# Reordering the start of a fused windowed-attention and feed-forward kernel: maxima one step ahead, early hidden slices in banks of their own, weights converted in another order

## The chip, the cores and the metric

The kernel runs on one core of one Trainium2 chip. The metric is device time in microseconds: the median of a few executions. One further execution was taken with the hardware profiler; all single durations come from it, and the profile's times count from the start of its span.

## What is computed

```python
# q, k, v: (8, 8, 576, 64); window = 32, dilation = 4
scores = (q @ k.T) / sqrt(64)
# heads 0-3: 0 <= i - j < 32;  heads 4-7: 0 <= i - j < 128 and (i - j) % 4 == 0
attn = softmax(where(mask, scores, -1e9))
x = (attn @ v).transpose(0, 2, 1, 3).reshape(4608, 512)   # tokens x model
h = x @ w_in                                              # w_in: 512 x 2048
g = maximum(h, 0) + alpha * minimum(h, 0)                 # alpha: one number per hidden unit
out = g @ w_out                                           # w_out: 2048 x 512
```

All is float32. Each large product is made of three matmuls in a rounded type (`PASSES`): every factor is split into a high part (rounded) and a low part (the rest), and high x high, high x low and low x high are added up in PSUM.

## The kernel before

**Work units.** A *pair* is two heads of one batch element: 32 pairs, 0 to 31, four (`NC`) for each batch element. A pair goes through `scores` (TensorE, 72 small matmul records, into two PSUM banks), `maxima` (VectorE: scale, mask, row maximum), `exponentials` (ScalarE, nine with their sums), `divisions` and `turns` (VectorE: divide, transpose), `values` (TensorE, into two banks), `highs` (ScalarE) and `lows` (VectorE), which write the split result into the token tiles x. Tokens come in nine tiles of 512.

**The feed-forward part** works in *slices* (t, f): token tile t, 128 hidden units f. `ffn_h` is 12 matmuls into one bank; `ffn_relu` makes two relus (ScalarE); `ffn_sum` joins them with alpha (VectorE); `ffn_high` (ScalarE) and `ffn_low` (VectorE) split g; `ffn_y` is 12 matmuls that add to four banks y. The list `slices` begins with (0, 0) to (0, 5) (`CUT` is 6), then (1, 0) to (1, 15), then the rest of tile 0 and tile 2. After slice 5 the four banks y are emptied: `end()` in `ffn_y` copies each to a buffer `o[c]` (ScalarE for c = 0 and 2, VectorE for c = 1 and 3) and stores it to `part`. It is called one step later, at n = 6, through `ended`.

**Weights** arrive as 64-bit numbers. One *conversion* (32 in all: `w_in` and `w_out`, 16 chunks each) is a load, `magnitude` (two ScalarE operations into a buffer `a`), `words` (two VectorE operations), `high` (ScalarE) and `low` (VectorE). `wq` sets their order, `taken` how many begin in each step. A conversion that begins in step n has its words and high in step n + 1 and its low in step n + 2 (lists `now` and `late`).

**Buffers around the change.** There are eight PSUM banks, a0 to a3 and y0 to y3; `bank` gives them out in turn. The tag "m" has five buffers of 128 x 512, used by the relu results, by the copies `o[c]`, and by the buffer `a` of conversions, unless `magnitude` takes `spare_a`:

```python
i = self.index                      # place in wq
if NC <= i < 2 * HALF and i % 2 == 0:       # NC = 4, HALF = 8
    self.a = spare_a[i // 2 % 2]
else:
    self.a = ffp.tile([P, DM], U32, tag="m", name=f"wa{self.id}", bufs=5)
```

**Order.** All five engines run in the order in which the program names their operations (`manual_schedule`); an operation waits only for its data and for its buffer to come free, and all behind it on its engine wait too. SP issues all DMAs. The start of the program handles pairs 0 to 4 in a loop over s, a loop over n = 0 to 5 the pairs up to 7 together with slices 0 to 5, and a loop over n from 6 on the other slices and more pairs. The last six token tiles follow in a stage of their own, which the change leaves as it is.

Of the kernel before, what the change touches and what calls it, by code (L numbers as in the profile page):

```python
# [15 lines left out]
ALU = mybir.AluOpType  # L16
# [37 lines left out]
def tile_window_attention_prelu_ffn(  # L54
# [34 lines left out]

    turn = {"a": 0, "y": 0, "g": 0}  # L90

    def bank(side, shape, name):
        n = turn[side]
        turn[side] = n + 1
        return psp.tile(shape, F32, tag=f"{side}{n % 4}", name=name)

    def gbuf(shape, dtype, name, i=None):
# [52 lines left out]
    class Pair:  # L150
        def __init__(self, b, c):
            self.b, self.c = b, c
            p = b * NC + c
            self.banks = "y" if p <= NC else "a"
            self.plain = 2 * c < HP
            self.mask = PLAIN if self.plain else DILATED
            self.id = f"{b}_{c}"
            self.pr = spare_pr[p % 2] if b < 2 else pr0
            self.room = rooms[c] if b < 2 else None
            self.sm = sums[p % 2]  # L160
# [63 lines left out]
        def values(self):  # L224


            self.po = [bank("a", [P, HB, BQ], f"o_{self.id}_{u}") for u in range(2)]
            for i in range(HB + 1):
                a, z = max(0, i - 1), min(HB, i + 1)
                for u in range(2):  # L230
                    if u == 0 and i == 0:
                        continue
                    for e in range(2):
                        rows = slice((2 * e + u) * BQ, (2 * e + u + 1) * BQ)
                        nc.tensor.matmul(  # L235
                            self.po[u][e * D:(e + 1) * D, a:z, :], lhsT=self.v[rows, i, :],
                            rhs=self.pt[rows, a * BK + (BQ if i else 0):z * BK - (BQ if i <= HB - 1 else 0)],
                            start=i == 1 - u, stop=i == HB, skip_group_check=True)
# [95 lines left out]


    gs, ys, ms = {}, {}, {}
    PASSES = ((0, 0), (0, 1), (1, 0))

    def ffn_h(t, f, first=0, end=NC):
        if first == 0:  # L340
            ms[t, f] = bank("a", [P, TT], f"h_{t}_{f}")
        for c in range(first, end):
            for n, (a, e) in enumerate(PASSES):
                nc.tensor.matmul(  # L344
                    ms[t, f], lhsT=weight(0, a, f)[:, c * P:(c + 1) * P], rhs=half(t, c)[:, e, :],
                    start=(c == 0 and n == 0), stop=(c == NC - 1 and n == 2))

    def ffn_relu(t, f):

        ps = ms[t, f]  # L350
        m = ffp.tile([P, TT], F32, tag="m", name=f"m_{t}_{f}", bufs=5)
        nc.scalar.activation(out=m, in_=ps, func=AF.Relu, scale=-1.0)
        nc.scalar.activation(out=ps, in_=ps, func=AF.Relu)
        ms[t, f] = ps, m

    def ffn_sum(t, f):
        ps, m = ms[t, f]
        nc.vector.scalar_tensor_tensor(
            out=m, in0=m, scalar=nal[:, f:f + 1], in1=ps, op0=ALU.mult, op1=ALU.add)
        ms[t, f] = m  # L360
# [8 lines left out]
    def ffn_high(t, f):  # L369
        g = gbuf([P, 2, TT], F32R, f"g_{t}_{f}")  # L370
        nc.scalar.copy(out=g[:, 0, :], in_=ms[t, f])  # L371
        gs[t, f] = g

    def ffn_low(t, f):
        g = gs[t, f]
        nc.vector.tensor_tensor(out=g[:, 1, :], in0=ms.pop((t, f)), in1=g[:, 0, :].bitcast(F32), op=ALU.subtract)

    def ffn_y(t, f):
        first = (t, f) in ((0, 0), (0, CUT), (1, 0), (2, HALF))
        if first:  # L380
            ys[t] = [bank("y", [P, TT], f"y_{t}_{f}_{c}") for c in range(NC)]
        g = gs.pop((t, f))
        cut, rest = (t, f) == (0, CUT - 1), t == 0 and f == NF - 1
        last = cut or (t, f) in ((0, NF - 1), (1, NF - 1), (2, HALF - 1))
        if last:
            o = [ffp.tile([P, TT], F32, tag="m", name=f"ob_{t}_{f}_{c}", bufs=5) for c in range(NC)]
        for c in range(NC):
            if rest:
                nc.sync.dma_start(out=o[c], in_=part[c])
            for n, (a, e) in enumerate(PASSES):  # L390
                nc.tensor.matmul(  # L391
                    ys[t][c], lhsT=weight(1, a, f)[:, c * P:(c + 1) * P], rhs=g[:, e, :],
                    start=(first and n == 0), stop=(last and n == 2),
                )

        def end():
            for c in range(NC):
                if rest:
                    nc.vector.tensor_tensor(out=o[c], in0=ys[t][c], in1=o[c], op=ALU.add)
                elif c % 2:  # L400
                    nc.vector.tensor_copy(out=o[c], in_=ys[t][c])
                else:
                    nc.scalar.copy(out=o[c], in_=ys[t][c])  # L403
                nc.sync.dma_start(
                    out=part[c] if cut else outT[c * P:(c + 1) * P, t * TT:(t + 1) * TT], in_=o[c])

        if last:
            ended.append(end)
# [363 lines left out]
    pairs = [Pair(b, c) for b in range(B) for c in range(NC)]  # L772


    wq = [(0, 0), (0, 1), (1, 0)]
    for f in range(1, NF):
        wq += [(0, f + 1), (1, f)] if f + 1 < NF else [(1, f)]
    order.update({w: i for i, w in enumerate(wq)})
    loads, convs = list(wq), list(wq)

    def load():
        if loads:
            load_weight(*loads.pop(0))
# [7 lines left out]
    def masks_of(kind):  # L791
        nc.sync.dma_start(out=mask_sb[:, kind:kind + HB], in_=masks[:, kind:kind + HB])
# [2 lines left out]
    pairs[0].load_qk()  # L795
    masks_of(PLAIN)
    load()
    nc.sync.dma_start(out=al, in_=alpha)
    pairs[1].load_qk()
    load()  # L800
    pairs[0].load_v()
    pairs[2].load_qk()
    load()
    pairs[1].load_v()
    masks_of(DILATED)
    pairs[3].load_qk()
    load()
    pairs[2].load_v()
# [5 lines left out]
    pairs[0].exponentials()  # L814
    for op in w.words():
        op()
    nc.vector.tensor_scalar_mul(nal, al, -1.0)
    nc.vector.tensor_scalar(out=bal, in0=al, scalar1=-1.0, scalar2=1.0, op0=ALU.mult, op1=ALU.add)
    w.high()
    before, w = w, conversion()  # L820
    for s in range(NC):
        u = pairs[s]
        pairs[s + NC].load_qk()
        load()
        if s + 1 == NC:
            ffn_h(0, 0, 0, 2)
            ffn_h(0, 1, 0, 2)
        pairs[s + 1].maxima()
        if s:
            pairs[s - 1].highs()  # L830
        pairs[s + 1].exponentials()
        if s:
            for op in w.words():
                op()
            w.high()
            later = conversion()
            pairs[s - 1].lows()
        u.divisions()
        u.turns()
        if s == 0:  # L840
            for op in w.words():
                op()
            w.high()
            later = conversion()
        before.low()
        before, w = w, later
        if s + 1 == NC:
            ffn_h(0, 0, 2, 3)
            ffn_h(0, 1, 2, 3)
        if s + 2 <= NC:  # L850
            pairs[s + 2].scores()
        u.values()
        pairs[s + NC].load_v()
    u, v = pairs[NC - 1], pairs[NC]
    u.highs()
    v.divisions()
    u.lows()
    for f in range(2):
        ffn_h(0, f, NC - 1, NC)
    v.turns()  # L860
    for op in w.words():
        op()
    ffn_relu(0, 0)
    ffn_relu(0, 1)
    before.low()
    w.high()
    load()
    late, now = [w], [conversion()]

    taken = [1, 2, 1, 1, 1, 2] + [1, 1, 2, 1, 1, 1, 2, 1, 1, 2, 1, 2, 1]  # L870

    def ahead():
        while taken and len(convs) - taken[0] < len(loads):
            load()

    for n in range(CUT):
        scored = pairs[NC + 1 + n] if n + 1 < NC else None
        valued = pairs[NC + n] if n < NC else None
        if n == 0:
            for f in range(2):  # L880
                ffn_sum(*slices[f])
        elif n > 1:
            ffn_sum(*slices[n])
        if scored:
            scored.scores()
        if valued:
            valued.values()
        if n:
            ffn_h(*slices[n + 1])
        ffn_high(*slices[n])  # L890
        if scored:
            scored.maxima()
            scored.exponentials(0, 5)
        ffn_low(*slices[n])
        if valued:
            valued.highs()
        if scored:
            scored.exponentials(5)
        if n:
            ffn_relu(*slices[n + 1])  # L900
        for w in now:
            for op in w.words():
                op()
        if valued:
            valued.lows()
        for w in late:
            w.low()
        if scored:
            scored.divisions()
            scored.turns()  # L910
        for w in now:
            w.high()
        late, now = now, [conversion() for _ in range(taken.pop(0))]
        ahead()
        if n:
            ffn_y(*slices[n - 1])

    score_at, value_at = {}, {}
    for p in range(2 * NC, AHEAD):
# [152 lines left out]
```

## Time and profile before

| | |
|---|---|
| median of 3 runs | 882.77 us (880.36 to 882.95) |
| profiled execution | 881.63 us, span 879.5 us |
| mean granted TensorE clock | 0.986 |
| TensorE busy | 850.5 us (97%), 8048 matmuls |
| VectorE busy | 536.1 us (61%), 901 instructions |
| ScalarE busy | 415.8 us (47%), 1150 instructions |
| GpSimd busy | 46.9 us (5%) |
| HBM read, written | 116.98 MB, 33.55 MB |

A row of the time line has the start in us, the duration in us, the engine, the line, the operation, output <- inputs, partitions x elements and type, the count, and in brackets the idle time before it with what ended it. A row of the chain has start, duration and what. The page shows each engine in 40 slices of 22 us, a digit being the busy share in tenths. "Granted clock" is the share of its full clock that TensorE had.

### The profile page before, as it was taken

What the parts mean: (1) busy time and instruction counts of PE and PEld (TensorE: products, weight loads), DVE (VectorE), ACT (ScalarE), POOL (GpSimd) and SP (SyncE); (2) the same over time, 40 slices, a digit from 0 to 9 for tenths busy, and PEclk for the clock granted to TensorE, in tenths of its full rate; (3) what the DMA queues carried; (4) which work ended last, traced back from release to release, by engine and by line L of the source; (5) the groups of instructions that cost most, each with busy time, mean ns of one, the idle gap of its engine ahead of it and who ended that gap; (6) DMA issues with size and microseconds to landing.
All of it is one profiled execution on the core that took longest, in us unless ns stands there. A gap on an engine that the chain in (4) does not pass through costs nothing.

```text
span 879.5 us, 19618 instructions
## 1 busy us (share of the span) xinstructions
PE 850.5 (97%) x8048; PEld 702.6 (80%) x8048; DVE 536.1 (61%) x901; ACT 415.8 (47%) x1150; POOL 46.9 (5%) x52
## 2 busy tenths in 40 slices
PE   4789999999999999999999999999999999999998
PEld 4577888888888788888888888888788888888886
DVE  6987677676776778674447665754277637304721
ACT  7886777534334344553446443643264226204500
POOL 0000000200504440000000000000000000000000
PEclk9779999999999999999999999999999999999999
DMA  9713344126889963765566666655475467435641
GB/s 338 250 67 120 120 162 144 48 95 208 270 294 313 286 192 124 240 179 151 163 178 198 172 175 193 192 145 158 113 193 145 147 194 194 121 96 172 182 126 48
DMA packets 95304, 151.81 MB, mean 173 GB/s; under 512 B 8432, under 2 KB 39152, under 8 KB 95216
## 3 DMA queue, kind: packets, MB, share of 16 engines
q1 hardware_dynamic: 95216, 150.57, 56.3%
q8 instruction: 63, 1.03, 0.5%
q14 instruction: 25, 0.20, 0.1%
HBM read 116.98 MB, written 33.55 MB: 171 GB/s over the span
## 4 chain that ended last, share of the span: by engine, by line
PE 95%; DMA 2%; issue 1%; DVE 1%; SPq 0%; ACT 0%; DVEq 0%
PE y L679 30%; PE h L344 15%; PE y L391 15%; PE pA L541 15%; PE pC L541 7%; PE o L235 5%; PE s L189 4%; PE pB L541 4%; DMA mask_sb<-masks 1%; DMA ws<-w_in 1%; DVE x L276 0%; DVE pt L222 0%; DVE wa L321 0%; DVE w_dt.float L197 0%; DVE w_dt.float L216 0%
## 5 line engine op out<-in xcount | busy, mean ns | idle before, releaser
L344 PE MATMUL h<-x,w_dt.float32r 128*128 128x512 f32 x576 | 144.5, 400 | 2.6 <-ACT x L271 1.2
L391 PE MATMUL y<-g,w_dt.float32r 128*128 128x512 f32 x576 | 138.7, 390 | 0.0
L344 PEld LDWEIGHTS h<-x,w_dt.float32r 128*128 128x128 f32 x576 | 109.0, 192 | 26.7 <-issue 1.6
L391 PEld LDWEIGHTS y<-g,w_dt.float32r 128*128 128x128 f32 x576 | 107.8, 188 | 23.0 <-ACT ob L403 0.4
L679 PE MATMUL y<-gp,ring_w 128*128 128x512 f32 x480 | 112.3, 390 | 0.0
L679 PEld LDWEIGHTS y<-gp,ring_w 128*128 128x128 f32 x480 | 89.7, 188 | 18.9
L679 PE MATMUL y<-gp,ring_xA 128*128 128x512 f32 x444 | 103.9, 390 | 0.0
L679 PEld LDWEIGHTS y<-gp,ring_xA 128*128 128x128 f32 x444 | 83.0, 188 | 17.6
L207 ACT ACTIVATE pr<-pr,nm 128x64 f32<-128x64 f32 x216 | 72.2, 336 | 45.7 <-DVE nm L200 45.7
L583 ACT COPY stage<-pA 128x512 f32<-128x512 f32 x72 | 42.3, 587 | 105.2 <-PE pA L541 105.2
L371 ACT CAST g<-m 128x512 fp32r<-128x512 f32 x48 | 29.7, 619 | 74.4 <-DVE m L366 71.6
L609 DVE TENSOR_TENSOR gp<-n,gp 128x512 fp32r<-128x512 f32 x96 | 63.2, 684 | 0.0
L601 DVE SCALAR_TENSOR_TENSOR n<-n,bal,stage 128x512 f32<-128x512 f32 x72 | 53.9, 749 | 13.9 <-ACT n L597 13.1
L541 PE MATMUL pA<-parts_w,ring_w 128*128 128x512 f32 x234 | 57.7, 390 | 0.7 <-ACT raw_xA L271 0.7
L605 ACT CAST gp<-n 128x512 fp32r<-128x512 f32 x96 | 56.6, 615 | 1.8 <-DVE n L601 1.8
L541 PE MATMUL pA<-parts_w,ring_xA 128*128 128x512 f32 x228 | 56.2, 390 | 0.5 <-ACT raw_xB L271 0.5
L679 PE MATMUL y<-gp,ring_g 128*128 128x512 f32 x228 | 54.5, 391 | 0.0
L541 PEld LDWEIGHTS pA<-parts_w,ring_w 128*128 128x128 f32 x234 | 43.8, 188 | 9.9 <-ACT raw_xA L271 0.8
L702 DVE TENSOR_TENSOR ob<-y,py 128x512 f32<-128x512 f32 x24 | 16.4, 691 | 57.8 <-PE y L679 57.8
L597 ACT ACTIVATE n<-stage 128x512 f32<-128x512 f32 x72 | 45.6, 633 | 12.5 <-DVE stage L590 12.0
L541 PEld LDWEIGHTS pA<-parts_w,ring_xA 128*128 128x128 f32 x228 | 42.7, 188 | 9.4 <-ACT raw_xB L271 0.6
L679 PEld LDWEIGHTS y<-gp,ring_g 128*128 128x128 f32 x228 | 42.5, 188 | 9.1
(96 smaller groups left out, 1139.8 us busy)
## 6 DMA issues: line engine op xcount, KB each, us to landing
ring_w<-wS SPq DMA_DIRECT2D x68, 256.0 KB, 2.9
ring_xA<-wS SPq DMA_DIRECT2D x67, 256.0 KB, 2.9
ring_w<-wO SPq DMA_DIRECT2D x40, 256.0 KB, 2.8
ring_xA<-wO SPq DMA_DIRECT2D x37, 256.0 KB, 2.7
out<-ob SPq DMA_DIRECT2D x36, 256.0 KB, 3.0
ring_g<-wS SPq DMA_DIRECT2D x33, 256.0 KB, 2.9
wO<-w_dt.float32r SPq DMA_DIRECT2D x32, 256.0 KB, 4.8
wS<-wc SPq DMA_DIRECT2D x16, 512.0 KB, 4.1
```

Source lines behind the costliest of these rows:

```text
L189: nc.tensor.matmul(self.ps[j // CUT0][m * BQ:(m + 1) * BQ, j % CUT0, :], lhsT=self.q[rows, n * BQ:(n + 1) * BQ], rhs=keys, start=True, sto ...
L207: nc.scalar.activation(out=self.pr[:, r, :], in_=self.pr[:, r, :], func=AF.Exp, bias=self.nm[:, r:r + 1], scale=1.0, accum_out=self.sm[:, ...
L235: nc.tensor.matmul(self.po[u][e * D:(e + 1) * D, a:z, :], lhsT=self.v[rows, i, :], rhs=self.pt[rows, a * BK + (BQ if i else 0):z * BK - (B ...
L344: nc.tensor.matmul(ms[t, f], lhsT=weight(0, a, f)[:, c * P:(c + 1) * P], rhs=half(t, c)[:, e, :], start=(c == 0 and n == 0), stop=(c == NC ...
L391: nc.tensor.matmul(ys[t][c], lhsT=weight(1, a, f)[:, c * P:(c + 1) * P], rhs=g[:, e, :], start=(first and n == 0), stop=(last and n == 2),)
L541: nc.tensor.matmul(to, lhsT=w[:, (2 * a + c) * P:(2 * a + c + 1) * P], rhs=part_of(name, e)[:, c * TT:(c + 1) * TT], start=start and c == ...
L583: nc.scalar.copy(out=self.s(n), in_=self.A)
L597: nc.scalar.activation(out=self.m[n], in_=self.at(n), func=AF.Relu, scale=-1.0)
L601: nc.vector.scalar_tensor_tensor(out=self.m[n], in0=self.m[n], scalar=bal[:, f:f + 1], in1=self.at(n), op0=ALU.mult, op1=ALU.add)
L605: nc.scalar.copy(out=self.g(n)[:, 0], in_=self.m[n])
L609: nc.vector.tensor_tensor(out=g[:, 1], in0=self.m.pop(n), in1=g[:, 0].bitcast(F32), op=ALU.subtract)
L679: nc.tensor.matmul(ys2[tt], lhsT=w[:, k * P:(k + 1) * P], rhs=g[:, e], start=j == 0 and n == 0, stop=j == GF - 1 and n == 2)
```

## The change

- `maxima` and `exponentials` of pairs 5, 6 and 7 come one step earlier: ahead of the `divisions` of the pair before. Their `scores` come earlier too, in the banks y.
- The h of slices 2 to 6 get banks a2 and a3 (`early`), values of pairs 4 to 7 banks a0 and a1. `ffn_h` runs up to three slices ahead of `ffn_y`.
- `wq` and `taken` change: chunks of `w_in` for tile 0 come first; two conversions a step from n = 2 to 5, then one and two in turn.
- Alpha is loaded and prepared later; the second set of masks is loaded one weight chunk and one v earlier.

```diff
-    def bank(side, shape, name):
-        n = turn[side]
-        turn[side] = n + 1
+    def bank(side, shape, name, n=None):
+        if n is None:
+            n = turn[side]
+            turn[side] = n + 1
...
-            self.banks = "y" if p <= NC else "a"
+            self.banks = "y" if p < 2 * NC else "a"
...
+                bank("a", [P, HB, BQ], f"o_{self.id}_{u}", u if NC <= self.p < 2 * NC else None) for u in range(2)]
...
+    early = [(0, f) for f in range(2, CUT)] + [(1, 0)]
...
+            ms[t, f] = bank("a", [P, TT], f"h_{t}_{f}", 2 + (t + f) % 2 if (t, f) in early else None)
...
-    wq = [(0, 0), (0, 1), (1, 0)]
-    for f in range(1, NF):
-        wq += [(0, f + 1), (1, f)] if f + 1 < NF else [(1, f)]
+    wq = [(0, 0), (0, 1), (1, 0), (0, 2), (0, 3), (0, 4), (1, 1), (0, 5)] + [(1, f) for f in range(2, CUT)]
+    wq += [(a, f) for f in range(CUT, NF) for a in range(2)]
...
-    nc.sync.dma_start(out=al, in_=alpha)          # was between the first two weight loads
+    masks_of(DILATED)                             # ahead of the third load; was behind v of pair 1
...
     for s in range(NC):
...
         if s + 1 == NC:
+            nc.sync.dma_start(out=al, in_=alpha)
             ffn_h(0, 0, 0, 2)
             ffn_h(0, 1, 0, 2)
...
-        if s + 2 <= NC:
-            pairs[s + 2].scores()
+        pairs[s + 2].scores()
         u.values()
...
     u.highs()
-    v.divisions()
+    pairs[NC + 1].maxima()
     u.lows()
     for f in range(2):
         ffn_h(0, f, NC - 1, NC)
+    v.divisions()
     v.turns()
     for op in w.words():
         op()
+    nc.vector.tensor_scalar_mul(nal, al, -1.0)
+    nc.vector.tensor_scalar(out=bal, in0=al, scalar1=-1.0, scalar2=1.0, op0=ALU.mult, op1=ALU.add)
     ffn_relu(0, 0)
     ffn_relu(0, 1)
+    pairs[NC + 2].scores()
     before.low()
+    pairs[NC + 1].exponentials()
     w.high()
...
-    taken = [1, 2, 1, 1, 1, 2] + [1, 1, 2, 1, 1, 1, 2, 1, 1, 2, 1, 2, 1]
+    taken = [1, 1, 2, 2, 2, 2] + [1, 2, 1, 2, 1, 2, 1, 2, 1, 2]
```

The loop over n from 0 to 5, new:

```python
for n in range(CUT):
    scored, divided, valued = (pairs[p] if p < 2 * NC else None for p in (NC + 2 + n, NC + 1 + n, NC + n))
    summed = [k for k in ((0, 1) if n == 0 else (n + 1,)) if k < CUT]
    if not divided:
        for w in late: w.low()
    for k in summed: ffn_sum(*slices[k])
    if valued: valued.values()
    if n == 0:
        ffn_h(*slices[2])
        pairs[2 * NC - 1].scores()
    if n < 2: ffn_h(*slices[n + 3])
    if summed: ffn_high(*slices[summed[0]])
    if scored: scored.maxima()
    if valued: valued.highs()
    if scored: scored.exponentials()
    if summed: ffn_low(*slices[summed[0]])
    if n == 0: ffn_high(*slices[1])
    if n + 2 < CUT or n + 1 == CUT: ffn_relu(*slices[min(n + 2, CUT)])
    for w in now:
        for op in w.words(): op()
    if valued: valued.lows()
    if divided:
        for w in late: w.low()
        divided.divisions(); divided.turns()
    if n == 0: ffn_low(*slices[1])
    for w in now: w.high()
    late, now = now, [conversion() for _ in range(taken.pop(0))]
    ahead()
    if n: ffn_y(*slices[n - 1])
    if n in (2, 3): ffn_h(*slices[n + 3])
```

More of the change, by code (lines that the diff above doesn't have):

```diff
@@ L152, in __init__ @@
             self.b, self.c = b, c
-            p = b * NC + c
-            self.banks = "y" if p <= NC else "a"
+            p = self.p = b * NC + c
+            self.banks = "y" if p < 2 * NC else "a"
             self.plain = 2 * c < HP
@@ L224, in values @@
         def values(self):
-            self.po = [bank("a", [P, HB, BQ], f"o_{self.id}_{u}") for u in range(2)]
+            self.po = [
+                bank("a", [P, HB, BQ], f"o_{self.id}_{u}", u if NC <= self.p < 2 * NC else None) for u in range(2)]
             for i in range(HB + 1):
@@ L340, in ffn_h @@
         if first == 0:
-            ms[t, f] = bank("a", [P, TT], f"h_{t}_{f}")
+            ms[t, f] = bank("a", [P, TT], f"h_{t}_{f}", 2 + (t + f) % 2 if (t, f) in early else None)
         for c in range(first, end):
@@ L802, in tile_window_attention_prelu_ffn @@
     pairs[2].load_qk()
+    masks_of(DILATED)
     load()
     pairs[1].load_v()
-    masks_of(DILATED)
     pairs[3].load_qk()
@@ L816, in tile_window_attention_prelu_ffn @@
         op()
-    nc.vector.tensor_scalar_mul(nal, al, -1.0)
-    nc.vector.tensor_scalar(out=bal, in0=al, scalar1=-1.0, scalar2=1.0, op0=ALU.mult, op1=ALU.add)
     w.high()
@@ L876, in tile_window_attention_prelu_ffn @@
     for n in range(CUT):
[L877 to L885, printed above, removed]
+        scored, divided, valued = (pairs[p] if p < 2 * NC else None for p in (NC + 2 + n, NC + 1 + n, NC + n))
+        summed = [k for k in ((0, 1) if n == 0 else (n + 1,)) if k < CUT]
+        if not divided:
+            for w in late:
+                w.low()
+        for k in summed:
+            ffn_sum(*slices[k])
         if valued:
             valued.values()
-        if n:
-            ffn_h(*slices[n + 1])
-        ffn_high(*slices[n])
+        if n == 0:
+            ffn_h(*slices[2])
+            pairs[2 * NC - 1].scores()
+        if n < 2:
+            ffn_h(*slices[n + 3])
+        if summed:
+            ffn_high(*slices[summed[0]])
         if scored:
             scored.maxima()
-            scored.exponentials(0, 5)
-        ffn_low(*slices[n])
         if valued:
@@ L897, in tile_window_attention_prelu_ffn @@
         if scored:
-            scored.exponentials(5)
-        if n:
-            ffn_relu(*slices[n + 1])
+            scored.exponentials()
+        if summed:
+            ffn_low(*slices[summed[0]])
+        if n == 0:
+            ffn_high(*slices[1])
+        if n + 2 < CUT or n + 1 == CUT:
+            ffn_relu(*slices[min(n + 2, CUT)])
         for w in now:
@@ L905, in tile_window_attention_prelu_ffn @@
             valued.lows()
[L906 to L910, printed above, removed]
+        if divided:
+            for w in late:
+                w.low()
+            divided.divisions()
+            divided.turns()
+        if n == 0:
+            ffn_low(*slices[1])
         for w in now:
@@ L916, in tile_window_attention_prelu_ffn @@
             ffn_y(*slices[n - 1])
+        if n in (2, 3):
+            ffn_h(*slices[n + 3])
     score_at, value_at = {}, {}
```

## The prediction

> **What bounds the kernel now.** I read the page's slices, the chain that ended last, the stretches, then each engine in order of time up to 101 us. First the row of slices; two stretches (window, length, busy us and count of PE, PE loads, VectorE, ScalarE, GpSimd, then granted clock, DMA share, GB/s); pieces of the chain (start, us, what):
>
> ```profile
> PE   4789999999999999999999999999999999999998
> 40.00:57.74 17.74, 13.15 (x309) 11.16 (x310) 16.57 (x36) 14.38 (x54) 0.00 (x0) 0.62 0.36 117
> 71.52:97.58 26.06, 26.06 (x185) 21.78 (x186) 17.12 (x28) 17.27 (x32) 0.00 (x0) 1.00 0.19 71
> ...
> 71.52 1.35 PE o L235 x70
> 81.27 2.72 PE y L391 x12
> 83.98 2.72 PE h L344 x12
> 97.58 3.08 PE y L391 x12
> 100.66 0.46 PE h L344 x2
> ```
>
> From 71.52 us TensorE is full at clock 1.00, and both kernels give it the same work. So the question is when it reaches the same place of its list. Before that VectorE is nearly full (16.57 of 17.74 us), and TensorE waits for it at clock 0.62. Slices are numbered as in `slices` (h6, y6 belong to slice 6), conversions c0, c1, ... in order of `wq`, pairs 0 to 7.
>
> **The start.** Alpha leaves the front of SP's queue and the dilated masks pass one weight load. That removes VectorE's wait for masks (first row). What is late next is the magnitude of c2: ScalarE ends it at 17.97 + 0.72 = 18.69, so words of c2 move from 18.87 only to 18.7, and all behind them by 0.2.
>
> ```profile
> 17.16 0.49 DVE L197 SCALAR_TENSOR_TENSOR w_dt.float<-s,mask_sb 128x320 f32<-128x320 f32 x1 [0.81 <-DMA mask_sb<-masks]
> 18.87 0.75 DVE L321 SCALAR_TENSOR_TENSOR wa<-ws,wa 128x512 uint16<-128x512 uint16 x1
> ...
> 17.97 0.72 ACT L314 ACTIVATE wa<-wa,least 128x512 int32<-128x512 int32 x1
> 43.09 0.60 ACT L329 CAST w_dt.float32r<-wa 128x512 fp32r<-128x512 f32 x1
> ...
> 36.71 1.35 PE L235 MATMUL o<-pt,w_dt.float 32*64 32x32 f32 x76
> 47.69 1.21 PE L189 MATMUL s<-w_dt.float 64*32 64x64 f32 x72
> ```
>
> Values of pair 3 ended at 36.71 + 1.35 = 38.06. Scores of pair 5 (1.2) now stand ahead of them: 39.1. Highs, lows, the last chunk of h0 and h1 and both relus follow as before, so relu 1 ends not at 43.1 but at 44.1. VectorE's maxima of pair 5 stand ahead of those lows, but end before highs are there; its divisions 4, words c5, the two alpha operations and sums are through by 46, under ScalarE's queue. The masks' and weights' DMAs land before their users; the weight behind the masks (c2) has until 17.28, where ScalarE now takes it.
>
> **ScalarE, then VectorE, to sum 5.** The durations are distances between starts (VectorE, then ScalarE), and one group row (busy, mean ns):
>
> ```profile
> 55.50 0.88 DVE L276 TENSOR_TENSOR x<-o,x 128x288 fp32r<-128x288 f32 x3
> 56.29 0.69 DVE L332 TENSOR_TENSOR w_dt.float32r<-w_dt.float,w_dt.float32r 128x512 fp32r<-128x512 f32 x1
> 62.41 0.49 DVE L197 SCALAR_TENSOR_TENSOR w_dt.float<-s,mask_sb 128x320 f32<-128x320 f32 x1 [1.59 <-PE s L189]
> 64.13 0.68 DVE L376 TENSOR_TENSOR g<-m,g 128x512 fp32r<-128x512 f32 x1
> 64.72 0.76 DVE L321 SCALAR_TENSOR_TENSOR w_dt.float<-w_dt.uint,w_dt.float 128x512 uint16<-128x512 uint16 x1
> 66.12 0.76 DVE L321 SCALAR_TENSOR_TENSOR wa<-w_dt.uint,wa 128x512 uint16<-128x512 uint16 x1
> 67.53 1.36 DVE L276 TENSOR_TENSOR x<-o,x 128x224 fp32r<-128x224 f32 x4
> 68.79 0.69 DVE L332 TENSOR_TENSOR w_dt.float32r<-wa,w_dt.float32r 128x512 fp32r<-128x512 f32 x1
> 69.39 0.17 DVE L214 TENSOR_SCALAR rs<-sums 128x9 f32<-128x9 f32 x1
> 71.34 0.70 DVE L358 SCALAR_TENSOR_TENSOR m<-m,nal,h 128x512 f32<-128x512 f32 x1
> ...
> 87.75 0.61 ACT L329 CAST w_dt.float32r<-w_dt.float 128x512 fp32r<-128x512 f32 x1
> 88.26 0.66 ACT L313 ACTIVATE wa<-w_dt.uint 128x512 f32<-128x512 bf16 x1
> 89.58 0.66 ACT L313 ACTIVATE w_dt.float<-w_dt.uint 128x512 f32<-128x512 bf16 x1
> 90.90 0.60 ACT L371 CAST g<-m 128x512 fp32r<-128x512 f32 x1
> 92.18 0.60 ACT L352 ACTIVATE m<-h 128x512 f32<-128x512 f32 x1 [0.68 <-PE h L344]
> 93.19 0.65 ACT L313 ACTIVATE wa<-w_dt.uint 128x512 f32<-128x512 bf16 x1
> ...
> L207 ACT ACTIVATE pr<-pr,nm 128x64 f32<-128x64 f32 x216 | 72.2, 336 | 45.7 <-DVE nm L200 45.7
> ```
>
> VectorE: lows 0.8 (three pieces) or 1.26 (four), maxima 1.72, low of a slice 0.6, words 1.4, low of a conversion 0.6, divisions and turns 1.95, sum 0.7. ScalarE: high of a conversion 0.5, magnitude 1.32, high of a slice 0.6 (0.5 where ScalarE goes on), relu 1.0, exponentials 9 x 0.336 = 3.0.
>
> ScalarE from 44.1: exponentials 5, high c5, magnitude c6, high 0 (now last) = 3.0 + 0.5 + 1.3 + 0.6, to 49.5. VectorE waits there for low 0, then:
> - n = 0: low 0, words c6, lows 4, low c5, divisions and turns 5, low 1: 5.95
> - n = 1: sum 2, maxima 7, low 2, words c7, lows 5, low c6, divisions and turns 6: 7.75
> - n = 2: sum 3, a wait of 0.6 for high 3, low 3, words c8, lows 6, low c7, divisions and turns 7: 7.1
> - n = 3: low c8, sum 4, the same wait 0.6, low 4, words c9 and c10, lows 7: 6.55
> - n = 4: low c9, low c10, sum 5: 1.9
>
> Together 29.2: sum 5 ends at 78.7. h5 and h6 both go to bank a3 (2 + (t + f) % 2 is 3 for both), so h6 waits for it, with y3, y4, h7 behind. Before h6 TensorE has done all up to y2 (turns 7 end near 70.3, then values 7 and y2, 1.3 + 2.7, to 74.7): it idles about 4 us. Before, h6 started at 83.98 with y3 already done; so to this place the change gains 83.98 - 78.7 - 2.72 = 2.5 us. The moved h's and scores themselves cost nothing more: they fill TensorE's idle time. If that cover is gone they cost 2.72 and 1.2 each.
>
> **The four copies of slice 5's sums, where I see the loss.** After y5 its four banks are copied to buffers o[0..3] and stored, and y6 needs the banks. The tag "m" has five buffers, shared by relus, these copies, and conversions (except even ones from c4 to c14, which use `spare_a`). In the kernel before, c13, c15 and relu 7 hold three at that place. Two are left, and that is what the trace shows: the third copy starts when the first store has landed, the fourth when the second has. (The last row is of the stores: us to landing.)
>
> ```profile
> 94.14 0.69 DVE L401 COPY ob<-y 128x512 f32<-128x512 f32 x1
> 95.54 0.57 ACT L403 COPY ob<-y 128x512 f32<-128x512 f32 x1
> ...
> 98.29 0.59 ACT L403 COPY ob<-y 128x512 f32<-128x512 f32 x1 [2.18 <-DMA part<-ob]
> 98.96 0.69 DVE L401 COPY ob<-y 128x512 f32<-128x512 f32 x1 [4.14 <-DMA part<-ob]
> ...
> DMA to landing us min/median/max: 2.0/2.1/2.3
> ```
>
> The new `taken` runs two conversions further. At n = 6 c15, c16, c17 and relu 7 hold four buffers: c16 is no longer under the even ones, and c15 and c16 get free only in n = 7, behind the copies in VectorE's queue. One buffer is left for four copies, so each waits for the store ahead of it.
>
> When the first can go: from 78.7 high 5 and low 5 (0.6 each), words c11 and c12 (2.8) to 82.7. Then ScalarE in order: high c12, magnitudes c13 and c14, relu 6, highs c13 and c14, magnitudes c15 and c16, high 6, relu 7, magnitude c17, highs c15 and c16 = 0.5 + 2.65 + 1 + 1 + 2.65 + 0.5 + 1 + 1.3 + 1 = 11.6, to 94.3; y5 is done by then (78.7 + 5 x 2.72 = 92.3). Then copy, store, copy, store, copy, store, copy: (0.58 + 2.18) + (0.69 + 2.2) + (0.58 + 2.18) + 0.69 = 9.1, to 103.4. y6's last three matmuls (2.72 / 4 = 0.7) end at 104.1, against 100.66 before. VectorE holds sum 7 and lows c15, c16 behind the last copy; y7 follows h9 at 106.8, and low 7 is there by then (0.7 + 1.2 + 0.8 + 0.6 after 103.4). The net is +3.5 us.
>
> **The clock.** TensorE is now idle for most of 95.7 to 103.4. Two stretches show what that does: with 1.40 us busy of 3.42 the clock is at 0.50 in the next; at 2.31 and even through the full third it stays there (1.00 after 57.74). With 1.76 of 3.41 it was kept (fourth row).
>
> ```profile
> 47.50:50.92 3.42, 1.40 (x87) 1.20 (x80) 3.32 (x9) 3.28 (x15) 0.00 (x0) 1.00 0.40 121
> 50.92:54.33 3.41, 2.31 (x77) 2.28 (x77) 3.31 (x8) 2.71 (x11) 0.00 (x0) 0.50 0.09 37
> 54.33:57.74 3.41, 3.41 (x10) 2.73 (x9) 3.31 (x9) 2.26 (x13) 0.00 (x0) 0.50 0.33 98
> 67.98:71.39 3.41, 1.76 (x8) 1.13 (x6) 3.31 (x10) 3.02 (x6) 0.00 (x0) 1.00 0.74 264
> ```
>
> With only y6's third part (0.7 us) in the 4.9 us ahead of 103.4, a drop is likely. The price is half of the time that work runs at 0.50: between 0 and 6.8 / 2 = 3.4 (both stretches from 50.92 to 57.74). The drop may come before the restart at 103.4, so I take little more than one stretch, 4 us: 2.0. A drop in h6's wait delays y5 by at most as much, to 94.3, where the first copy stands anyway: nothing.
>
> The Trainium skill ("TensorE: Matmul & The Clock Gate", section "Why this matters for your kernels") says the clock falls back after a PE-idle gap of over about 3 us. The gaps inside y6 are about 2.2 us each, so by that rule the 2.0 fall away and the sum is 3.5. The trace is nearer to a share of a fixed window: by 50.92 the idle stretch was 2.0 us old and the clock fell.
>
> **The sum.** -2.5 at h6, then +3.5 at y6's end (in which that is contained), +2.0 clock: 881.63 + 5.5 = 887.1 for the profiled execution. That lies 1.1 below the median of the runs and 0.3 below the mean of all four times known; I say 887.5. Unknown: stores of 2.0 to 2.3 us (0.3), VectorE's waits (1 both ways), the clock at scores 5 (0 to 2.6, the fourth rival; I take 0, as the six h matmuls ahead of them run at full clock), the clock at y6 (0 to 3.4).
>
> **Rivals.** Measurement can tell 0.3%, that is 880.1 and 885.4.
> - *The buffers suffice* (two or more free at the copies, as before). y6 waits as little as before, and the 2.5 us remain, less 0 to 2 for a clock lost in h6's 4 us wait: 879.1 to 881.1. For it: the order of `taken` may leave a buffer that I count as held. Against: c15 to c17 and relu 7 all have later readers. It decides as soon as the second copy starts without a store landed. Chance 0.15.
> - *The chain of stores starts earlier* (ScalarE not behind): first copy at y5's end, 92.3, y6 ends at 102.1, +1.4, clock kept: 883.1. For it: before, ScalarE had idle time there. Chance 0.13.
> - *The clock is kept* (the rule of the gap): 885.1 to 885.5. Against: the row of 50.92. Chance 0.17.
> - *The early order does not work*: at clock 0.50 scores 5 and values 3 take twice their 1.21 + 1.35 us, and lows 3 and all behind them move by 2.6: 890.1. For it: 0.62 as the mean clock of that part. Chance 0.05.
> - The forecast: 0.5, own range 884.5 to 891.
>
> Range 882 to 891: it leaves out the first rival's better part. Faster 0.1 (two thirds of the first), same 0.27 (the rest of it, the second, half of the third), slower 0.63.
>
> **What would show it.** Right: TensorE busy but for short waits until y2, about 4 us idle before h6 released by sum 5 (scalar_tensor_tensor of m, nal, h), h6 near 78.7; four copies of ob each 2.8 us behind the last, the first near 94.3, each released by a store of part; y6 torn into four; clock 0.50 for a few us near 104. Wrong: two copies without a wait, or copies 1 and 2 close together; h6 later than 81, or y6 in one piece.

## The result, and the profile after

The changed kernel takes 889.53 us (median of 4 runs, 888.02 to 891.35) against 881.98 us (880.36 to 882.95) before: 1.0088 times as long, 95% interval 1.0062 to 1.0114. It is slower, by 7.5 us. The profiled execution took 889.72 us with a span of 887.6, 8.1 more than the 879.5 before.

TensorE's row of slices and the row of its clock, from the page of the changed kernel. The fourth digit was 9 before and is 8 now, the fifth was 9 and is 7; all other slices of TensorE stand as they did. One slice is 22.2 us, so the fourth is 66.6 to 88.8, with h6's wait, and the fifth 88.8 to 110.9: the stretch of the four copies.

```profile
PE   4788799999999999999999999999999999999998
PEclk9899799999999999999999999999999999999999
```

The chain that ended last, changed kernel, pieces around that stretch (start, us, what):

```profile
90.41 2.73 PE h L347 x12
...
93.66 0.60 ACT h L356
...
95.61 1.03 ACT w_dt.float32r L331 x2
96.64 0.49 ACT ob L406
...
97.14 2.98 DMA part<-ob
...
100.25 0.70 DVE ob L404
...
100.97 2.01 DMA part<-ob
...
103.13 0.59 ACT ob L406
...
103.75 1.99 DMA part<-ob
...
106.23 0.70 DVE ob L404
...
106.98 1.65 PE y L394 x3
108.63 4.50 PE h L347 x12
113.13 2.72 PE y L394 x12
```

Before the change the chain here was TensorE alone. Now from 96.64 to 106.93 it is copy, store, copy, store, copy, store, copy: every copy starts when the store of the copy ahead of it has landed, the last one 0.49 us behind the landing, the others within 0.15. TensorE in order of time, changed kernel (start, us, then the count of matmuls, the idle time ahead and what ended it):

```profile
36.94 1.21 PE L190 MATMUL s<-w_dt.float 64*32 64x64 f32 x72
38.08 1.03 PE L237 MATMUL o<-pt,w_dt.float 32*64 32x32 f32 x52
40.08 0.55 PE L237 MATMUL o<-pt,w_dt.float 32*64 32x64 f32 x24 [0.97 <-issue]
...
80.31 4.46 PE L347 MATMUL h<-x,w_dt.float32r 128*128 128x512 f32 x12 [3.63 <-DVE m L361]
...
98.41 0.84 PE L394 MATMUL y<-g,w_dt.float32r 128*128 128x512 f32 x3
101.00 0.96 PE L394 MATMUL y<-g,w_dt.float32r 128*128 128x512 f32 x3 [1.75 <-DVE ob L404]
103.77 1.65 PE L394 MATMUL y<-g,w_dt.float32r 128*128 128x512 f32 x3 [1.81 <-ACT ob L406]
106.98 1.65 PE L394 MATMUL y<-g,w_dt.float32r 128*128 128x512 f32 x3 [1.56 <-DVE ob L404]
```

h6 waits 3.63 us for sum 5, and y6 is torn into its four groups of three matmuls, each behind one copy. y6 ends at 106.98 + 1.65 = 108.63 (100.66 before) and y7 starts at 113.13. Before, it started 2.72 after y6's end, at 103.4: 9.7 us later. The clock accounts for part of that. Windows of the changed kernel (length, busy us and count of PE, PE loads, VectorE, ScalarE, GpSimd, granted clock, DMA share, GB/s):

```profile
78.14:81.55 3.41, 1.24 (x5) 1.05 (x6) 2.71 (x6) 2.71 (x5) 0.00 (x0) 1.00 0.56 171
81.55:84.96 3.41, 3.41 (x9) 2.65 (x8) 3.34 (x6) 1.13 (x2) 0.00 (x0) 0.50 0.23 73
...
98.62:102.03 3.41, 1.59 (x6) 0.67 (x4) 0.69 (x1) 0.00 (x0) 0.00 (x0) 1.00 0.28 105
102.03:112.27 10.24, 6.94 (x16) 4.98 (x16) 5.03 (x8) 5.14 (x9) 0.00 (x0) 0.50 0.25 84
```

From 106.98 to 113.13 TensorE ran y6's last three matmuls and the twelve of h9 in 6.15 us, which take 3.4 at full clock (12 take 2.72): 2.75 us lost.

Of the 9.7 us, 1.6 come back behind this place. The waits of TensorE from 114 us on show 1.2 of them: these two rows of the kernel before have no counterpart in the changed one. The other 0.4 I could not place.

```profile
PE pA L541 <- ACT raw_xA L271: 0.7, 1, 0.7
PE pA L541 <- ACT raw_xB L271: 0.5, 1, 0.5
```

### The profile page after: what moved, and what is told of

It reads as the page before. It is cut to its first block, busy times and chain, and to the rows that moved or that the text cites. A ratio compares the mean times of both kernels' runs of the same rounds, so it can differ in the third digit from the quotient of the medians.

```text
span 887.6 us, 19630 instructions
## 1 busy us (share of the span) xinstructions
PE 853.1 (96%) x8048; PEld 702.5 (79%) x8048; DVE 536.5 (60%) x901; ACT 415.9 (47%) x1150; POOL 47.0 (5%) x52
## 4 chain that ended last, share of the span: by engine, by line
PE 91%; DVE 4%; ACT 3%; DMA 1%; issue 1%; SPq 0%; DVEq 0%; ACTq 0%
PE y L682 30%; PE pA L544 15%; PE h L347 14%; PE y L394 13%; PE pC L544 7%; PE o L237 4%; PE pB L544 4%; PE s L190 3%; ACT w_dt.float L208 1%; DMA part<-ob 1%; DVE x L278 1%; DMA ws<-w_in 1%; DVE w_dt.float32r L334 0%; DVE pt L223 0%; DVE w_dt.float L217 0%
## 5 line engine op out<-in xcount | busy, mean ns | idle before, releaser
L347 PE MATMUL h<-x,w_dt.float32r 128*128 128x512 f32 x576 | 147.4, 406 | 6.4 <-DVE m L361 3.6
L394 PE MATMUL y<-g,w_dt.float32r 128*128 128x512 f32 x576 | 140.9, 394 | 5.1 <-DVE ob L404 3.3
L347 PEld LDWEIGHTS h<-x,w_dt.float32r 128*128 128x128 f32 x576 | 110.9, 195 | 31.9 <-DVE m L361 4.1
L394 PEld LDWEIGHTS y<-g,w_dt.float32r 128*128 128x128 f32 x576 | 108.6, 190 | 29.2 <-DVE ob L404 4.5
L586 ACT COPY stage<-pA 128x512 f32<-128x512 f32 x72 | 42.4, 589 | 103.4 <-PE pA L544 103.4
```

The source lines that it names most:

```text
L347: nc.tensor.matmul(ms[t, f], lhsT=weight(0, a, f)[:, c * P:(c + 1) * P], rhs=half(t, c)[:, e, :], start=(c == 0 and n == 0), stop=(c == NC ...
L394: nc.tensor.matmul(ys[t][c], lhsT=weight(1, a, f)[:, c * P:(c + 1) * P], rhs=g[:, e, :], start=(first and n == 0), stop=(last and n == 2),)
L586: nc.scalar.copy(out=self.s(n), in_=self.A)
```

## The experiments

The theory was that one free buffer of tag "m" at the four copies costs all of the loss. The first rival was that the loss lies ahead of the copies (VectorE's and ScalarE's list, h6's wait, the lost clock), the second that it lies behind them. Times are medians; ratios are to the kernel before, run beside it.

**own_buffers.** The changed kernel, with the four copies of slice 5's sums in buffers of attention tags that are free there.

```diff
-            o = [ffp.tile([P, TT], F32, tag="m", name=f"ob_{t}_{f}_{c}", bufs=5) for c in range(NC)]
+            if cut:
+                o = [att.tile([P, n], F32, tag=g, name=f"ob_{t}_{f}_{g}")[:, :TT]
+                     for g, n in (("k", S), ("q", S), ("v", (HB + 1) * D), ("pt", HB * BK))]
+            else:
+                o = [ffp.tile([P, TT], F32, tag="m", ...) for c in range(NC)]
```

> The changed kernel, but the four copies of slice 5's sums go to four buffers of their own (those of k, q, v and the transposed rows, idle at that time). Theory (one free buffer of five makes each copy wait for the store ahead of it): no copy waits for a store, y6 runs in one piece from about 98.5 us, the clock stays at 1.00 there, and the 9.1 us between y7's start (113.1) and 101.3 + 2.7 go: about 880.5 us, range 879.5 to 882.5. Rival (VectorE and ScalarE are late with their queues, the stores only stand beside that): the copies still come 2 to 3 us apart and the time stays over 886.

Measured: 881.89 us (12 runs), ratio 1.0008 [0.9995, 1.0022]. The whole loss is gone and no gain is left. TensorE's rows of this kernel:

```profile
81.03 4.60 PE L347 MATMUL h<-x,w_dt.float32r 128*128 128x512 f32 x12 [3.68 <-DVE m L361]
...
99.09 2.88 PE L397 MATMUL y<-g,w_dt.float32r 128*128 128x512 f32 x12
```

h6 still waits 3.68 us and still runs at the lower clock (4.60 instead of about 2.9), but y6 is in one piece. What lies ahead of the copies is the same as in the changed kernel, and so is what lies behind, so both rivals fall.

**one_conversion_less.** The changed kernel, with one conversion put off, so that c17 holds no buffer at the copies.

```diff
-    taken = [1, 1, 2, 2, 2, 2] + [1, 2, 1, 2, 1, 2, 1, 2, 1, 2]
+    taken = [1, 1, 2, 2, 2, 1] + [1, 2, 1, 2, 1, 2, 1, 2, 1, 2, 1]
```

> The changed kernel, with one conversion less begun in step 5 (taken 1 1 2 2 2 1 and then 1 and 2 in turn, to the same 32). Theory: c15, c16 and relu 7 hold three of the five buffers at the copies, two are free as in the kernel before, so copies 1 and 2 start without a store, copies 3 and 4 wait once; y6 loses under 1.5 us, clock kept: about 881, range 880 to 883. Rival (the early order itself, h ahead or maxima ahead, is what costs): no change against the changed kernel, over 886.

Measured: 882.71 us (12 runs), 1.0017 [1.0002, 1.0032]. It takes one digit of the list (and a 1 at its end, for the conversion that was put off) to remove the loss: with two buffers instead of one, two copies go ahead without a store, and y6 is whole:

```profile
81.89 3.06 PE L347 MATMUL h<-x,w_dt.float32r 128*128 128x512 f32 x12 [3.66 <-DVE m L361]
...
98.38 2.90 PE L394 MATMUL y<-g,w_dt.float32r 128*128 128x512 f32 x12
```

The clock is the surprise. Ahead of h6 stands nearly the same wait as in own_buffers (3.66 against 3.68 us), but the clock is kept: 3.06 us for the same twelve matmuls against 4.60. The last section comes back to it.

**before_two_more.** The kernel before, with only its list of conversions lengthened by two ahead of the copies.

```diff
-    taken = [1, 2, 1, 1, 1, 2] + [1, 1, 2, 1, 1, 1, 2, 1, 1, 2, 1, 2, 1]
+    taken = [1, 2, 1, 2, 2, 2] + [1, 1, 2, 1, 1, 1, 2, 1, 1, 2, 1, 1]
```

> The kernel before, with nothing changed but two conversions more begun by step 5 (taken 1 2 1 2 2 2, then 1 1 2 1 1 1 2 1 1 2 1 1), so that c15, c16, c17 and relu 7 hold four of the five buffers at the copies. Theory: the loss comes with this list alone: four copies in a chain of about 10 us from about 96, y6's end near 107 against 100.66, clock lost after it: 890, range 887 to 893. Rival (the loss needs the new order of scores, maxima and h): no change, 882.

Measured: 891.32 us (6 runs), 1.0108 [1.0089, 1.0126]. The loss comes without any other part of the change, and the picture is the same, y6 in its four groups of three, each behind a copy:

```profile
99.98 0.96 PE L391 MATMUL y<-g,w_dt.float32r 128*128 128x512 f32 x3 [1.20 <-ACT ob L403]
102.82 1.65 PE L391 MATMUL y<-g,w_dt.float32r 128*128 128x512 f32 x3 [1.87 <-DVE ob L401]
105.53 1.65 PE L391 MATMUL y<-g,w_dt.float32r 128*128 128x512 f32 x3 [1.06 <-ACT ob L403]
108.43 1.65 PE L391 MATMUL y<-g,w_dt.float32r 128*128 128x512 f32 x3 [1.25 <-DVE ob L401]
```

**two_more_own_buffers.** The same lengthened list, and the four buffers of own_buffers (its diff on top of the last one).

> before_two_more with the four copies in buffers of their own (those of k, q, v and the transposed rows). Theory (the longer list costs only by the fourth buffer it holds at the copies): all of the 9 us go, 882, range 881 to 883.5. Rival (two conversions more by step 5 also cost as work of ScalarE and VectorE): it stays over 884.

Measured: 883.17 us (12 runs), 1.0009 [0.9996, 1.0023]. By the two ratios the longer list costs 9.5 us with shared buffers and 0.8, no more than can be told from nothing, without; a wait of y6 of 1.15 us for ScalarE's first copy is left there. So it is the buffers, not the work in the list.

**h9_ahead_of_y6.** The changed kernel, with TensorE doing h9 ahead of y6, so that the wait for the copies has 2.7 us of work in it.

```diff
-        if n + 1 < NS and not whole:
+        if n + 1 < NS and not whole and n != 8:
             ffn_h(*slices[n + 1])
+        if n == 7:
+            ffn_h(*slices[9])
```

> The changed kernel, but TensorE does h9 ahead of y6, and so in the wait for the four copies. Theory (y6's 10 us are a wait for buffers that leaves TensorE idle, and a clock that falls for it): the copies' chain stays as it is, 2.72 us of work fill idle time, and with them the stretch from 98.6 to 102 is full, so the clock falls later or not at all ahead of y6's end: 2.7 to 5 us less than the changed kernel, 885.5, range 884 to 887. Rival (the loss is work, not waiting): no change, 889.5.

Measured: 890.72 us (6 runs), 1.0092 [1.0069, 1.0114]: a miss, nothing gained. VectorE's rows of this kernel, then TensorE's, then ScalarE's relu 7:

```profile
108.21 0.69 DVE L404 COPY ob<-y 128x512 f32<-128x512 f32 x1 [5.29 <-DMA part<-ob]
...
111.29 0.68 DVE L379 TENSOR_TENSOR g<-m,g 128x512 fp32r<-128x512 f32 x1
```

```profile
108.95 0.97 PE L394 MATMUL y<-g,w_dt.float32r 128*128 128x512 f32 x3 [2.25 <-DVE ob L404]
110.26 0.54 PE L394 MATMUL y<-g,w_dt.float32r 128*128 128x512 f32 x1 [0.34 <-ACT g L374]
112.03 5.06 PE L394 MATMUL y<-g,w_dt.float32r 128*128 128x512 f32 x11 [1.23 <-DVE g L379]
...
95.10 0.60 ACT L355 ACTIVATE m<-h 128x512 f32<-128x512 f32 x1 [0.85 <-PE h L347]
```

VectorE stands 5.29 us in front of its last copy, with sum 7 and low 7 queued behind it. With h9 gone from there, y7 follows y6 at once and meets that queue: it waits 0.34 us for high 7 and 1.23 for low 7. I had costed the copy's place on VectorE for y6 alone. The clock was not saved either: it fell at 110.56 for 6.83 us, and y7's last eleven matmuls took 5.06 us. This execution also lost the clock for 6.83 us, not 3.41, behind h6's wait; relu 7 then waited 0.85 us for h7, and the first copy came at 98.47, not 96.54. So the runs do not separate how much of the miss is which.

The other question was where the gain of the early order went: the forecast had 2.5 us at h6, the trace 0.95.

**start_alone.** The kernel before, with only the start of the change: alpha later, masks earlier.

```diff
-    nc.sync.dma_start(out=al, in_=alpha)
...
+    masks_of(DILATED)
     load()
     pairs[1].load_v()
-    masks_of(DILATED)
...
         if s + 1 == NC:
+            nc.sync.dma_start(out=al, in_=alpha)
```

> The kernel before with only the edits of the start: alpha loaded and prepared later, the second masks one weight load and one v earlier. Theory (the wait for masks, 0.81 us, passes to the magnitude of c2): 0.2 us less, within 0.5 of the kernel before. Rival (VectorE's list really starts 0.8 us earlier): 0.8 to 1 us less.

Measured: 881.59 us (12 runs), 0.9994 [0.9982, 1.0005]. As forecast the wait for the second masks is replaced by one for ScalarE's magnitude of c2, as this row of VectorE shows. It starts at 19.40, not earlier than the 18.87 before: in this execution ScalarE could begin on the first weight chunk only at 8.34, against 7.67 in the kernel before.

```profile
19.40 0.74 DVE L321 SCALAR_TENSOR_TENSOR wa<-ws,wa 128x512 uint16<-128x512 uint16 x1 [0.74 <-ACT wa L314]
```

**values_first.** own_buffers, with values 3 ahead of scores 5, and lows 3 ahead of maxima 5.

```diff
-        pairs[s + 2].scores()
+        if s + 1 < NC:
+            pairs[s + 2].scores()
         u.values()
+        if s + 1 == NC:
+            pairs[s + 2].scores()
...
-    pairs[NC + 1].maxima()
     u.lows()
+    pairs[NC + 1].maxima()
```

> As own_buffers, and in the last step of the first loop values of pair 3 stand ahead of scores of pair 5, and lows of pair 3 ahead of maxima of pair 5 (their order in the kernel before). Theory (in the changed kernel values 3 ended at 40.6 against 38.1 before, half of that behind the scores and half in a stop of 0.97 us in their middle, and ScalarE's chain from relu to high 0 and VectorE's list behind it move along): low 0, sum 5 and h6 come about 2 us earlier than in own_buffers, and so the end: about 878.5, range 877.5 to 880. Rival (VectorE's list is as long whatever its start, since maxima 5 now come later): same time as own_buffers.

Measured: 880.56 us (12 runs), 0.999 [0.998, 1.0001]; expected was at most 880, so this is a miss. In its trace h6 starts at 79.00, 2.0 us earlier than in own_buffers, and y6 at 97.07 instead of 99.09, as the theory had it. The medians differ by only 1.3, the spans of the two profiled executions by 0.5 (878.4 against 878.9). Of the 1.5 us missing there, one idle stop of 1.06 us at 513 us, for which the profile shows no wait, takes most; whether all runs have it is open. The stop of 0.97 us inside values 3 has not gone but sits in scores 5 now:

```profile
40.57 0.54 PE L190 MATMUL s<-w_dt.float 64*32 64x64 f32 x24 [1.43 <-issue]
...
79.00 4.62 PE L347 MATMUL h<-x,w_dt.float32r 128*128 128x512 f32 x12 [3.68 <-DVE m L361]
```

**h6_behind_y3.** values_first, with h6 issued behind y3 instead of ahead of it, so that y3 fills the wait for sum 5.

```diff
-        if n in (2, 3):
-            ffn_h(*slices[n + 3])
+        if n == 2:
+            ffn_h(*slices[5])
+        if n == 4:
+            ffn_h(*slices[6])
```

> As values_first, and TensorE does h6 behind y3 and not ahead of it. Theory (h6 waits 3.7 us for bank a3, which sum 5 frees, and y3, y4 and h7 stand behind it with nothing to wait for but lows c9 and c10): y3 starts at about 75.2 us behind y2, waits once for low c9 (near 77.7), and ends near 80.2; h6 follows without a wait; the clock does not fall at 79. y4 starts near 83 against 86.3: about 3 us less, 877.3, range 876 to 879. Rival (VectorE's list sets the pace there, whatever TensorE does first): less than 0.8 us, over 879.5.

Measured: 879.29 us (12 runs), 0.9973 [0.996, 0.9986]: 1.3 gained on values_first, less than expected and just outside the range. Part of y3's work went into the wait, but then y3 itself waits:

```profile
77.98 3.88 PE L397 MATMUL y<-g,w_dt.float32r 128*128 128x512 f32 x10 [1.87 <-DVE w_dt.float32r L334]
```

It needs the low part of c9, which stands near the end of VectorE's list, with only the low of c10 between it and sum 5, and the clock still fell (1.54 us busy from 75.50 to 78.91, then 0.50).

**list_alone.** The changed kernel with shared buffers, and a list with one conversion less at n = 2, which shortens VectorE's list ahead of sum 5 as well as freeing buffers.

```diff
-    taken = [1, 1, 2, 2, 2, 2] + [1, 2, 1, 2, 1, 2, 1, 2, 1, 2]
+    taken = [1, 1, 1, 2, 2, 2] + [1, 2, 1, 2, 1, 2, 1, 2, 1, 2, 1]
```

> The changed kernel with one number of its list changed: taken 1 1 1 2 2 2 and then 1 and 2 in turn; the copies share the five buffers again. Theory: at the copies c15, c16 and relu 7 hold three buffers, so copies 1 and 2 go at once and y6 loses about 1 us in place of 8 with the clock; and sum 5 comes 2 us earlier, h6's wait falls under 2 us and the clock is kept there. From own_buffers (881.9) less 3.5 for the second, plus 1 for the first: 879.4, range 878 to 881. Rival (only the buffers matter, h6's wait does not): 882 to 883, as one_conversion_less.

Measured: 880.27 us (12 runs), 0.9983 [0.9971, 0.9995]. One number of the list (and a 1 at its end) takes 9.3 us off the changed kernel. TensorE: h6 is 2.0 us earlier, its wait 1.65 instead of 3.63, and y6 is in two pieces, not four:

```profile
78.29 3.03 PE L347 MATMUL h<-x,w_dt.float32r 128*128 128x512 f32 x12 [1.65 <-DVE m L361]
...
95.63 1.66 PE L394 MATMUL y<-g,w_dt.float32r 128*128 128x512 f32 x6 [0.71 <-ACT ob L406]
98.36 1.76 PE L394 MATMUL y<-g,w_dt.float32r 128*128 128x512 f32 x6 [1.07 <-ACT ob L406]
```

**one_less_at_2.** The same list on top of values_first.

> As values_first, with one conversion begun at n = 2 in place of two (taken 1 1 1 2 2 2, then 1 and 2 in turn to the same 32). Theory (VectorE's two words of c9 and c10 and two lows stand ahead of sum 5): its list to sum 5 is 1.4 + 0.6 us shorter, h6 starts 2 us earlier (near 77), the wait ahead of it falls under 2 us and the clock is kept (1.7 us): 877.0, range 876 to 879. Rival (the work comes back in the next steps, and y4 or y5 waits for c10 and c11): as values_first, 880.5.

Measured: 877.07 us (6 runs), 0.9943 [0.9928, 0.9958], 3.5 less than values_first; h6 starts at 77.04 after a wait of 1.70 and the clock is kept.

**both_moves.** The same list and h6_behind_y3 together.

> h6_behind_y3 and one_less_at_2 together. Theory (both fill the same wait ahead of h6): no sum of the two; y3 ends near 78.6, h6 near 81.3, y4 then waits for low c10 until near 82: within 0.8 us of the better of the two. Rival (they are separate gains): 3 us below the better one.

Measured: 876.62 us (6 runs), 0.9938 [0.9923, 0.9953]. The two do not add up, since both fill the same wait. What TensorE waits for next is y6's first copy, 1.25 us, which is what the last run takes up.

**copies_first.** both_moves, and ScalarE's highs of the last two conversions moved behind its copies of slice 5's sums.

```diff
-            for w in late:
-                w.high()
+            if n != CUT:
+                for w in late:
+                    w.high()
...
         while ended:
             ended.pop()()
+        if n == CUT:
+            for w in late:
+                w.high()
```

> both_moves, with ScalarE's two highs of step 6 behind the copies of slice 5 and not ahead of them. Theory (y6 waits 1.25 us for ScalarE's first copy, which stands behind two highs of 0.5 us each though y5 is done): y6 starts 1.0 us earlier: 875.6, range 874.8 to 876.4. Rival (the highs that come later are waited for by lows, and y7 waits in y6's place): as both_moves, 876.6.

Measured: 876.14 us (6 runs), 0.9933 [0.9917, 0.9948]: the fastest of all, 0.7% below the kernel before, though on both_moves (876.62) the gain is inside the spread of the runs. y6's first group in both_moves, then in copies_first:

```profile
94.29 3.01 PE L397 MATMUL y<-g,w_dt.float32r 128*128 128x512 f32 x12 [1.25 <-ACT ob_k L409]
```

```profile
93.12 3.03 PE L397 MATMUL y<-g,w_dt.float32r 128*128 128x512 f32 x12 [0.18 <-ACT ob_k L409]
```

So the changed kernel is 5.6 us faster than the kernel before (881.72 - 876.14), once four buffers are found for the copies, one conversion is put off, values 3 and lows 3 are back in their old order, and h6 and two of ScalarE's highs are moved. How much of this the early order gives is not shown: the kernel before was not run with repairs of that kind. With the shorter list alone (list_alone) the changed kernel is 1.5 us faster than the kernel before, 0.9983 [0.9971, 0.9995].

## Why the prediction was right

The forecast was 887.5 us, in a range of 882 to 891; the median is 889.53. The mechanism that carried it, one free buffer for four copies, is shown from three sides: its own buffers take the loss away, one conversion less takes it away, and the list alone brings it into the kernel before. The size was 2 us short. In the trace y7 starts 9.7 us late where the steps gave 5.5, and these are the terms:

- **The start**: right in kind (the wait for the masks became one for ScalarE; start_alone moved the time by nothing that can be told). But words of c2 start at 19.10, not 18.7: in this execution ScalarE begins on the first weight chunk at 8.04, against 7.67 before. That start varies from 7.67 to 8.54 over all traces, with and without the change.
- **Values 3 at 39.1**: mis-sized. They ended at 40.08 + 0.55 = 40.63. 0.97 of the miss is the stop in the middle of them, which the forecast had not and whose cause the profile does not name; 0.2 is the late start (scores 5 begin at 36.94, where values 3 began at 36.71); and 38.06 + 1.2 is 39.3, not 39.1. So the low of slice 0 began at 50.86, not 49.5.
- **VectorE's list, 29.2 us, and h6's wait of 4**: right. It took 29.4 (50.86 to 80.26, the first and last of VectorE's rows below) and h6 waited 3.63. With the late start the gain at h6 is 83.98 - 80.31 - 2.72 = 0.95, not 2.5: +1.55.

```profile
50.86 0.69 DVE L379 TENSOR_TENSOR g<-m,g 128x512 fp32r<-128x512 f32 x1 [1.10 <-ACT g L374]
...
79.51 0.75 DVE L361 SCALAR_TENSOR_TENSOR m<-m,nal,h 128x512 f32<-128x512 f32 x1
```

- **VectorE's and ScalarE's lists from sum 5 to the first copy, 15.6**: mis-sized. It came 16.3 us behind sum 5 (80.26 to 96.54): +0.7. VectorE's part, up to words c12, took 0.2 more than counted; highs c13 and c14 took 1.27 (88.61 to 89.88) and not 1.0, since the second begins at 89.35, behind words c14, which end at 89.31; high 6 took 0.63 and not 0.5. The rest is hundredths.
- **"A drop in h6's wait costs nothing"**: right within 0.1, but by luck. The clock fell there, h6 took 4.46 us, and h7 ended at 93.14. I had costed only y5, which the copies wait for (h8, behind it, starts at 95.69, before the first copy), and not h7, for which ScalarE's relu 7 waits. But ScalarE's high 6 ended at 92.53 + 0.61 = 93.14 too, so relu 7 would have begun at most 0.1 earlier, as these rows show. In h9_ahead_of_y6, where the clock stayed down twice as long, relu 7 did wait, 0.85 us.

```profile
92.53 0.61 ACT L374 CAST g<-m 128x512 fp32r<-128x512 f32 x1
93.16 0.60 ACT L355 ACTIVATE m<-h 128x512 f32<-128x512 f32 x1
```

- **The chain of copies, 9.1 us**: right in kind, short by 1.3. It took 10.4 (96.54 to 106.93). From the end of one copy to the start of the next it was 3.13, 2.19 and 2.51 us, where I had taken 2.18, 2.2 and 2.18 from the rows before. The first store needed 2.98 us to land, the other two 2.01 and 1.99, and the last copy began 0.49 behind the third landing, for which the chain names nothing that it waited for.
- **The clock, 2.0**: it fell as forecast, at 102.03, and cost 2.75: +0.75. The work that counted at 0.50 was 5.3 us long (106.98 to 112.27), not 4.

These add to 4.3, and 5.5 + 4.3 is 9.8 against 9.7 measured. That 1.6 come back later was no step of mine: it is luck that it brings the time nearer to the forecast than the steps were.

Of the rivals, the buffers did not suffice, and the chain did not start earlier. "The clock is kept" fell by the trace: the gaps inside y6 are 1.75, 1.81 and 1.56 us, and 98.62 to 102.03 was busy for 1.59 of 3.41 us, yet the clock went to 0.50 at 102.03. The rule of the Trainium skill ("TensorE: Matmul & The Clock Gate", section "Why this matters for your kernels") asks for an idle gap of over about 3 us, and there was none; the measurement decides. The order's own rival, clock 0.50 at scores 5 and values 3, did not come: the two rows at 36.94 and 38.08 run at full rate, and what delayed them was the stop.

Still open: what the stops of 0.97 and 1.43 us inside the small matmuls are; why the changed kernel has no waits for raw_xA and raw_xB; and how the miss of h9_ahead_of_y6 divides between low 7, the clock behind y6 and the longer loss of clock behind h6.

## What to carry to other kernels

Before a list of background work is lengthened, count at each place behind it how many buffers of every shared tag are held and until when: one buffer fewer (one free instead of two) turned two pairs of copies into a single chain of copy and store, 10.4 us long, on two engines that had other work queued behind. A wait is worth filling only where the inputs of what moves into it, and of what then follows, do not stand behind the same late instruction (y3's c9 in h6_behind_y3, low 7 in h9_ahead_of_y6). And where a clock that may fall is costed, ask of every engine whether its list waits for the slowed matmuls, not only of the one that comes next on the path: relu 7 waited for h7 by 0.1 us at most in the changed kernel, but by 0.85 in h9_ahead_of_y6.

## What the runs showed of the hardware

Within one trace the changes of the granted clock lie multiples of 3.41 us apart (81.55, 84.96, 102.03, 112.27 in the changed kernel), but at another phase in each execution. That fits the two waits of 3.66 and 3.68 us ahead of h6. In own_buffers the wait fell mostly into one such window, and the clock dropped behind it; in one_conversion_less, whose changes (42.65, 46.06, 59.71, 63.12) put the border at 80.19, it is split over two, and the clock was kept. The windows of own_buffers, then of one_conversion_less:

```profile
78.41:81.82 3.41, 0.79 (x3) 0.67 (x4) 2.71 (x7) 3.17 (x6) 0.00 (x0) 1.00 0.73 216
81.82:85.23 3.41, 3.41 (x9) 2.63 (x8) 3.34 (x6) 0.68 (x2) 0.00 (x0) 0.50 0.13 22
```

```profile
76.78:80.19 3.41, 1.44 (x7) 0.86 (x5) 3.38 (x8) 2.60 (x6) 0.00 (x0) 1.00 0.48 154
80.19:83.60 3.41, 1.72 (x7) 1.42 (x8) 2.71 (x5) 2.27 (x4) 0.00 (x0) 1.00 0.56 154
```

So by these two traces, whether a wait of that length costs the clock depends on the phase of that execution; the price was 1.6 us here (h6's start to y6's start is 18.06 us in own_buffers and 16.49 in the other). The busy share of the window is not the whole rule: 1.44 of 3.41 was kept here, and 1.59 dropped in the changed kernel. How long the clock stays down varied too: 3.41 us, 6.83 (h9_ahead_of_y6, behind h6's wait) and 10.24 (the changed kernel). In these three it came back at the end of the first such window that TensorE filled. The busy times of the windows at 0.50 are 3.41 in own_buffers, 1.84 and 3.42 in h9_ahead_of_y6, and 1.65, 1.87 and 3.42 in the changed kernel. So in the changed kernel the waits inside y6 not only lost the clock but kept it down until a whole window behind them was full.
